# Converting a unit's blocks of g to hi and lo one unit later in the program text

## The chip, the core and the metric

The kernel runs on one core of a Trainium2 chip. The metric is the time of one execution in device microseconds (us); smaller is better. The core's engines run side by side, each taking its own instructions in order: PE (TensorE, matrix products into PSUM), ACT (ScalarE), DVE (VectorE), POOL (GpSimd, which cannot reach PSUM) and SP, which issues the DMA transfers.

## The reference

Attention in chunks of 64 tokens, then a feed-forward layer with the activation h - tanh(h), all in float32:

```python
scores = scale * np.matmul(q_c, k_c.transpose(0, 1, 2, 4, 3))   # chunks of 64 x 64
scores = scores - np.max(scores, axis=-1, keepdims=True)
attn = np.exp(scores)
attn = attn / (np.sum(attn, axis=-1, keepdims=True) + 1e-09)
out = np.matmul(attn, v_c)
...
h = x @ w_in          # x: 4608 x 512, w_in: 512 x 2048
g = h - np.tanh(h)
return (g @ w_out).astype(np.float32)   # w_out: 2048 x 512
```

q, k and v are 8 batches x 8 heads x 576 tokens x 64.

## The kernel before

The 4608 tokens are cut into nine groups of 512. Groups 0 to 2 run the feed-forward layer in a plain form (`FeedForward`); groups 3 to 8 run it in the class `Fast`, which the change touches. While a group's feed-forward layer runs, the attention of the next group is computed in between: `interleaved` puts its parts (splits of q, k and v into two float16 halves, scores, exponents, normalisation, a transposition by DMA, values) into lists `at[...]` that the loop of `Fast.run` calls at set steps.

To keep float32 accuracy with float16 products, each operand is held as two float16 numbers, "hi" (the rounded value) and "lo" (the rest).

A group in `Fast` is worked in 16 units: two halves `b` of 256 tokens, times eight pairs `j` of hidden blocks. One step `s` of `Fast.run` handles a unit:

- `gemm1` (L576): the first layer, 24 matmuls of 256 columns into one PSUM buffer `ph` (there are two).
- `shrink`: tanh on ACT (L584), `u` = h - tanh(h) on DVE (L585), three sums on POOL (L586 to L588) that make seven blocks out of the four of `u` (as in Strassen's scheme, seven products stand for eight), hi on ACT (L589) and lo on DVE (L590). `u` has two places; hi and lo have five sets of places, used in turn. The unit then goes into `queue`.
- the attention parts in `at[2 * s]`.
- `gemm2` (L607): the second layer, 21 matmuls, of the unit at the head of the queue, once more than `FAST_LAG` = 3 are queued: the unit of three steps earlier. When the unit at the head is the first of a half (`j == 0`), one step is left out and the next step runs two second layers.
- the attention parts in `at[2 * s + 1]`.

The second layer's products of a half add up in four PSUM tiles `po`. After the eighth unit of a half, `gemm2` calls `finish` (L611 to L633): two activations on ACT (L622 of the first PSUM tile, L623 of half the second), six scalar-tensor-tensor adds on DVE (all at L620, in the helper `add`), two subtractions or additions on POOL (L625 and L631), and two output DMAs. The next half's first second layer writes the same PSUM tiles, so it waits for these reads. With the lag of three, the finish of a group's first half falls in step 10 and that of its second half in step 2 of the next group; the last one falls behind the last unit.

In this part of the kernel the order on each engine is not written out by hand. The program text gives each instruction a rank; when the program is built, a planner goes through it with a clock of its own and sets the order in every engine's queue. On the chip each engine then keeps to that order. The lines of other work that share the engines with the units: L107, L124 (largest values of the next group's q, k and v), L114 (a reduction over partitions on POOL), L297 and L298 (splits into hi and lo), L308 (attention products), L321 to L323 (maxima, differences, exponents), L329 to L340 (normalisation, and hi and lo of the weights), L348 (the transposing DMA), L360 and L361 (attention's result).

Of the kernel before, what the change touches and what calls it, by code (L numbers as in the profile page):

```python
# [17 lines left out]
AF = mybir.ActivationFunctionType  # L18
ALU = mybir.AluOpType
# [3 lines left out]
P = 128  # L23
# [14 lines left out]
MOST = max(SIZES) * P  # L38
LAG = 2
FAST = 3  # L40
FAST_LAG = 3
RAW = 3
WS = 2
EARLY_FC = 8
# [15 lines left out]
def attn_ffn_kernel(ctx: ExitStack, tc: tile.TileContext, qE, kE, vE, qL, kL, vL, w_in, w_out, out):  # L60
# [8 lines left out]
    nc = tc.nc  # L69
    scale = 1.0 / math.sqrt(D)  # L70
# [18 lines left out]
    def place_of(a, part, fc, dtype=F16):  # L89

        return w_pool[fc].tile([P, DM], F32R, name=f"w{a}{part}{fc}").bitcast(dtype)
# [66 lines left out]
    class Early:  # L158
# [3 lines left out]
        def __init__(self, pool, psum, bufs, zeros):  # L162
            self.pool, self.psum, self.st, self.bufs = pool, psum, defaultdict(dict), bufs
            self.qbd, self.vbd = (
                [pool.tile([P, 4, P, 2], F32, name=f"{n}{i}", bufs=1) for i in range(bufs)] for n in ("qbd", "vbd")
            )
            for i in range(bufs):
                for t in self.qbd[i], self.vbd[i]:
                    for r, o in ((slice(0, D), slice(D, P)), (slice(D, P), slice(0, D))):
                        if t is self.qbd[i]:  # L170
                            nc.vector.memset(t[r, :, o], 0.0)
                        else:
                            nc.scalar.copy(out=t[r, :, o], in_=zeros[r].rearrange("p (hp d two) -> p hp d two", hp=4, two=2))
# [78 lines left out]
    class Late:  # L252
# [31 lines left out]
        def split(self, g, b, n):  # L284

            d, to = self.st[g, b], self.st[f"g{g}"]["to"][:, "qkv".index(n):"qkv".index(n) + 1]
            d["exp"] = self.st[f"g{g}"]["exp"]
            raw = self.raw[n][:, 2 * b:2 * b + 2].rearrange("p e n -> p (e n)")
            if n == "k":
                hl = self.k16  # L290
                if hl is None:
                    t = self.pool.tile([P, 2, 2 * H * CH], F16, name="a", bufs=1)
                    hl = t[:, 0], t[:, 1]
                d["k"] = hl
            else:
                hl = self.q16 if n == "q" else self.v16
            nc.scalar.activation(hl[0], raw, AF.Copy, scale=to)  # L297
            nc.vector.scalar_tensor_tensor(out=hl[1], in0=raw, scalar=to, in1=hl[0], op0=ALU.mult, op1=ALU.subtract)  # L298
# [172 lines left out]
    class FeedForward:  # L471
# [27 lines left out]
        def shrink(self):  # L499
            fc, t0, t1, n, ph = self.ph  # L500
            t = ffn.tile([P, MOST], F32, name="t", bufs=3)[:, :n]
            if self.half:
                nc.scalar.activation(t, ph, AF.Tanh, scale=self.sig)
                nc.vector.scalar_tensor_tensor(out=t, in0=ph, scalar=self.sig, in1=t, op0=ALU.mult, op1=ALU.subtract)  # L504
            else:
                nc.scalar.activation(t, ph, AF.Tanh)
                nc.vector.tensor_sub(t, ph, t)
            gh = ffn.tile([P, MOST], F32R, name="gh")[:, :n]
            gl = ffn.tile([P, MOST], F32R, name="gl")[:, :n]
            nc.scalar.copy(out=gh, in_=t)  # L510
            nc.vector.tensor_sub(gl, t, gh)  # L511
            self.queue.append((fc, t0, t1, (gh, gl)))
# [36 lines left out]
    class Fast:  # L549
# [5 lines left out]
        SUM = {7: 0, 3: 1, 4: 2, 6: 3, 5: 4, 2: 5, 1: 6}  # L555

        def __init__(self, pools):
            self.pools, self.queue, self.units, self.po = pools, [], 0, None
            u = xpool.tile([P, KC, MOST], F32R, name="xl").bitcast(F32).rearrange("p a n -> p (a n)")
            self.u = [u[:, i * 8 * P:i * 8 * P + 7 * P].rearrange("p (s n) -> p s n", n=P) for i in range(2)]  # L560
            tiles = [ffn.tile([P, MOST], F32R, name=f"g{a}").bitcast(F16) for _ in range(2) for a in "hl"] + g_tiles
            self.g = [[t[:, :7 * P].rearrange("p (s n) -> p s n", n=P) for t in tiles[2 * i:2 * i + 2]] for i in range(FAST_LAG + 2)]

# [13 lines left out]
                        k += 1  # L577

        def shrink(self, b, j):
            sig, to = self.powers[:2]  # L580
            t = ffn.tile([P, MOST], F32, name="t", bufs=3).rearrange("p (s n) -> p s n", n=P)
            u, (gh, gl) = self.u[self.units % 2], self.g[self.units % len(self.g)]
            self.units += 1
            nc.scalar.activation(t, self.ph, AF.Tanh, scale=sig)  # L584
            nc.vector.scalar_tensor_tensor(out=u[:, :4], in0=self.ph, scalar=sig, in1=t, op0=ALU.mult, op1=ALU.subtract)  # L585
            nc.gpsimd.tensor_add(u[:, 4:6], u[:, 1:3], u[:, 0:4:3])  # L586
            nc.gpsimd.tensor_add(u[:, 6], u[:, 1], u[:, 2])  # L587
            nc.gpsimd.tensor_sub(u[:, 0:4:3], u[:, 0:2], u[:, 2:4])  # L588
            nc.scalar.activation(gh, u, AF.Copy, scale=to)  # L589
            nc.vector.scalar_tensor_tensor(out=gl, in0=u, scalar=to, in1=gh, op0=ALU.mult, op1=ALU.subtract)  # L590
            self.queue.append((b, j, gh, gl, self.powers, self.row + 2 * b * P))

        def first_next(self):
            return self.queue[0][1] == 0
# [40 lines left out]
        def run(self, g, x, at):  # L635
            self.group(g, x)
            waited = False
            for s in range(2 * FC // 2):
                unit = divmod(s, FC // 2)
                self.gemm1(*unit)  # L640
                self.shrink(*unit)
                for f in at.pop(2 * s, []):
                    f()
                if len(self.queue) > FAST_LAG:
                    if self.first_next() and not waited:
                        waited = True
                    else:
                        waited = False
                        self.gemm2()
                        if len(self.queue) > FAST_LAG and not self.first_next():  # L650
                            self.gemm2()
                for f in at.pop(2 * s + 1, []):
                    f()
            for k in sorted(at):
                for f in at[k]:
                    f()

        def drain(self):
            while self.queue:
                self.gemm2()  # L660

# [2 lines left out]
    outs, g_tiles, post = [], [], []  # L664
# [63 lines left out]
    pools = []  # L728
# [17 lines left out]
    att, half, over = Late(late), Half(late), defaultdict(list)  # L746
    for g in range(1, NG):
        x, nx = nx, new_half_x() if g + 1 < NG else None
        at = interleaved(att, g + 1, nx) if nx else {}
        if g == 1:  # L750
            half.powers()
            first_place = late.tile([P, DM], F32, name="first_place", bufs=1).bitcast(F16)
            for fc in range(FC):

                at[2 * fc + 1].append(lambda fc=fc: half.convert(fc, place_of("l", 0, fc - 1) if fc else first_place))

            def more(k):

                if k == 0:
                    t = [place_of("h", 0, fc) for fc in range(4)]  # L760
                    att.q16, att.v16 = t[0:2], t[2:4]
                else:
                    outs.extend(place_of("h", 0, fc, F32) for fc in range(4, 8))
                    g_tiles.extend(place_of("h", 0, fc) for fc in range(8, 12))
                    half.free = [("h", 0, 12), ("h", 0, 13), ("h", 0, 14), ("h", 0, 15)]

            at[8].insert(0, lambda: more(0))
            at[2 * FC + 2].append(lambda: more(1))
        if g < FAST:
            if g == FAST - 1:  # L770
                for j in range(FC // 2):
                    at[4 * j + 7].append(lambda j=j: half.combine(j))
                    k = 4 * j + 9
                    (at if k < 2 * (FC + LAG) else over)[k].append(lambda j=j: half.shorten(j))
            order = range(FC) if g < FAST - 1 else [j + f * FC // 2 for j in range(FC // 2) for f in range(2)]
            ff = FeedForward(g, x)
            ff.room(ps_o1, range(2))
            ff.room(ps_o2, range(2, SIZES[g]))
            ff.run([(fc, 0, SIZES[g]) for fc in order], at)
            continue  # L780
        if g == FAST:
            for fs in over.values():
                for f in fs:
                    f()
            post.extend(place_of(*n, F32) for n in half.free[:3])
            g_tiles.extend(place_of(*n) for n in half.free[3:5])
            fast = Fast((ps_o1, ps_o2))
        fast.run(g, x, at)
    fast.drain()
# [46 lines left out]
```

## Time and profile before

| | |
|---|---|
| median of three runs | 953.4 us (952.98 to 954.25) |
| the profiled execution | 954.0 us, span of the profile 952.2 us |
| `Fast` on the time line | from about 348 us to the end |
| granted clock of TensorE, mean | 0.971 |
| busy share of the span: PE, DVE, ACT, POOL | 89%, 64%, 50%, 28% |

Times on a time line are microseconds from the span's start. A row of a time line has the start, the duration, the engine, the line, the operation with its output and inputs, shapes, and in brackets how long the engine sat idle before it and what ended that. Neighbouring instructions of an engine overlap a little: the next one starts some 0.1 us ahead of the end of the last. A row of waits has who waited, for whom, the sum in us, how many times, and the longest. A row of windows has a stretch, its length, the busy time and the number of instructions of PE, weight loads, DVE, ACT and POOL, then the granted clock, the DMA engines' share and GB/s. In the names, hi and lo lie in tiles `gh`, `gl`, `wh` or `wl`, and `u` in `xl`.

### The profile page before, as it was taken

How to read it: one execution, taken by the hardware profiler on the slowest of the kernel's cores; microseconds unless marked ns; L12 is line 12 of the kernel's file. 1: busy time of each engine (PE TensorE's matmuls, PEld its weight loads, DVE VectorE, ACT ScalarE, POOL GpSimd, SP SyncE). 2: the span in 40 equal slices, each digit the busy share in tenths (PEclk: the TensorE clock that was granted, in tenths of full speed). 3: DMA queues.
4: the chain of work that ended last, by engine and by line, in shares of the span. 5: the costliest groups of instructions: out<-in, count | busy, mean ns of one | idle time of the engine just before them, and what ended most of it. 6: DMA issues, size and time to landing. Idle time of an engine off the chain costs nothing.

```text
span 952.2 us, 19954 instructions
## 1 busy us (share of the span) xinstructions
PE 847.2 (89%) x8525; PEld 694.3 (73%) x8525; DVE 606.1 (64%) x878; ACT 472.9 (50%) x767; POOL 268.9 (28%) x375
## 2 busy tenths in 40 slices
PE   8999999999998768887887989879887889889997
PEld 5888778887665557776776877768776678778886
DVE  6987978776787756565646556565646555554343
ACT  7796967656454634335443543335433534433332
POOL 0000000000455463232423242332323242333342
PEclk9999999999999979999998999999999999999999
DMA  8764433113120322103021122112130101010000
GB/s 260 216 188 168 142 126 118 47 43 108 50 67 1 63 72 40 52 24 89 31 60 45 24 67 67 45 45 67 46 60 31 23 23 23 2 46 4 21 23 23
DMA packets 61400, 63.14 MB, mean 66 GB/s; under 512 B 32640, under 2 KB 40832, under 8 KB 61312
## 3 DMA queue, kind: packets, MB, share of 16 engines
q1 hardware_dynamic: 61312, 61.88, 22.4%
q8 instruction: 66, 1.08, 0.5%
q14 instruction: 22, 0.18, 0.1%
HBM read 45.09 MB, written 9.44 MB: 57 GB/s over the span
## 4 chain that ended last, share of the span: by engine, by line
PE 30%; DVE 28%; POOL 16%; ACT 12%; DMA 7%; issue 5%; SPq 2%; ACTq 0%; DVEq 0%; POOLq 0%
PE ph L495 10%; PE po L519 10%; DVE xl L585 5%; POOL xl L586 5%; POOL xl L588 5%; ACT wh L589 4%; DMA s<-a 4%; PE po L607 4%; DVE wh L590 4%; PE ph L576 3%; POOL xl L587 3%; ACT gh L589 3%; DVE gl L590 3%; DVE wh L298 2%; DVE a L298 1%
## 5 line engine op out<-in xcount | busy, mean ns | idle before, releaser
L576 PE MATMUL ph<-xh,wl 128*128 128x256 f16 x2160 | 262.2, 280 | 38.5 <-DVE xl L585 38.4
L576 PEld LDWEIGHTS <-wl 128*128 128x128 f16 x2160 | 215.8, 100 | 72.5 <-issue 42.2
L586 POOL TENSOR_TENSOR xl<-xl 128x256 f32<-128x256 f32 x96 | 69.5, 724 | 346.9 <-DVE xl L585 290.9
L590 DVE SCALAR_TENSOR_TENSOR wh<-xl,to_g,wh 128x896 f16<-128x896 f32 x57 | 66.5, 1167 | 130.0 <-ACT wh L589 130.0
L607 PEld LDWEIGHTS <-wh 128*128 128x128 f16 x1197 | 120.7, 101 | 36.3 <-issue 18.9
L589 ACT ACTIVATE wh<-xl,to_g 128x896 f16<-128x896 f32 x57 | 59.4, 1042 | 172.6 <-POOL xl L588 167.3
L607 PE MATMUL po<-wl,wh 128*128 128x256 f16 x642 | 107.2, 277 | 10.9 <-DVE wh L620 7.4
L607 PE MATMUL po<-wh,wh 128*128 128x256 f16 x555 | 105.8, 288 | 4.3 <-DVE wh L620 4.3
L590 DVE SCALAR_TENSOR_TENSOR gl<-xl,to_g,gh 128x896 f16<-128x896 f32 x39 | 46.3, 1187 | 84.7 <-ACT gh L589 84.7
L589 ACT ACTIVATE gh<-xl,to_g 128x896 f16<-128x896 f32 x39 | 40.6, 1042 | 117.9 <-POOL xl L588 112.7
L519 PE MATMUL po<-wh,gh 128*128 128x512 f32 x192 | 79.4, 414 | 4.4 <-ACT gh L510 4.4
L585 DVE SCALAR_TENSOR_TENSOR xl<-ph,sig,t 128x512 f32<-128x512 f32 x96 | 70.9, 739 | 18.5 <-ACT t L584 18.5
L495 PE MATMUL ph<-xh,wl 128*128 128x512 f16 (+2 forms) x324 | 77.0, 375 | 4.3 <-DVE t L504 3.2
L519 PE MATMUL po<-wh,gl 128*128 128x512 f32 x192 | 76.3, 401 | 0.5 <-DVE gl L511 0.4
L519 PE MATMUL po<-wl,gh 128*128 128x512 f32 x192 | 76.0, 396 | 0.0
L588 POOL TENSOR_TENSOR xl<-xl 128x256 f32<-128x256 f32 x96 | 70.5, 735 | 0.0
L607 PEld LDWEIGHTS <-gh 128*128 128x128 f16 x546 | 54.2, 100 | 19.0 <-issue 11.9
L584 ACT ACTIVATE t<-ph,sig 128x512 f32<-128x512 f32 x96 | 64.4, 671 | 1.0 <-PE ph L576 1.0
L607 PE MATMUL po<-wl,gh 128*128 128x256 f16 x292 | 45.4, 276 | 7.0 <-DVE wh L620 4.7
L511 DVE TENSOR_TENSOR gl<-t,gh 128x512 fp32r<-128x512 f32 (+1 forms) x52 | 37.4, 720 | 19.5 <-ACT gh L510 17.3
L587 POOL TENSOR_TENSOR xl<-xl 128x128 f32<-128x128 f32 x96 | 48.3, 504 | 0.0
L519 PEld LDWEIGHTS po<-wh,gh 128*128 128x128 f32 x192 | 36.5, 190 | 14.1 <-ACT gh L510 5.8
(146 smaller groups left out, 1409.5 us busy)
## 6 DMA issues: line engine op xcount, KB each, us to landing
raw<-w_in SPq DMA_DIRECT2D x16, 512.0 KB, 3.7
raw<-w_out SPq DMA_DIRECT2D x16, 512.0 KB, 5.5
out<-wh SPq DMA_DIRECT2D x32, 256.0 KB, 2.0
rawk<-kL SPq DMA_DIRECT2D x28, 256.0 KB, 3.3
rawv<-vL SPq DMA_DIRECT2D x28, 256.0 KB, 3.0
xl<-qL SPq DMA_DIRECT2D x28, 256.0 KB, 2.8
qbd<-qE SPq DMA_DIRECT2D x16, 128.0 KB, 4.3
k<-kE SPq DMA_DIRECT2D x8, 256.0 KB, 4.8
```

What stands on the lines that cost most here:

```text
L495: nc.tensor.matmul(ph, lhsT=self.weight(fc, 0, a)[:, kc * P:(kc + 1) * P], rhs=x[b][:, kc, cols], start=(k == 0), stop=(k == 3 * KC - 1))
L511: nc.vector.tensor_sub(gl, t, gh)
L519: nc.tensor.matmul(self.po[t], lhsT=gg[a][:, ts], rhs=self.weight(fc, 1, b), start=(fc == 0 and i == 0), stop=(fc == FC - 1 and i == 2))
L576: nc.tensor.matmul(self.ph[:, 1 - f::2, :], lhsT=half_w[fc][:, w, kc * P:(kc + 1) * P], rhs=rhs, start=(k == 0), stop=(k == 3 * KC - 1))
L584: nc.scalar.activation(t, self.ph, AF.Tanh, scale=sig)
L585: nc.vector.scalar_tensor_tensor(out=u[:, :4], in0=self.ph, scalar=sig, in1=t, op0=ALU.mult, op1=ALU.subtract)
L586: nc.gpsimd.tensor_add(u[:, 4:6], u[:, 1:3], u[:, 0:4:3])
L587: nc.gpsimd.tensor_add(u[:, 6], u[:, 1], u[:, 2])
L588: nc.gpsimd.tensor_sub(u[:, 0:4:3], u[:, 0:2], u[:, 2:4])
L589: nc.scalar.activation(gh, u, AF.Copy, scale=to)
L590: nc.vector.scalar_tensor_tensor(out=gl, in0=u, scalar=to, in1=gh, op0=ALU.mult, op1=ALU.subtract)
L607: nc.tensor.matmul(place[m], lhsT=part[:, self.SUM[m]], rhs=w[m][:, o], start=first, stop=(j == FC // 2 - 1 and part is gl), skip_group_ch ...
```

## The change

`shrink` ends after the three sums and keeps the unit in `ready`. A new function `split` makes hi and lo of the kept unit and puts it into the queue. In `run`, the step of a unit first issues the unit's own first layer, tanh, u and sums, then `split` for the unit before; the attention parts and the second layer follow as they did. `drain` splits the last unit. `FAST_LAG` goes from 3 to 2, so the second layer of a unit stays at the same step, and the sets of places for hi and lo go from five to four; two tiles that served the fifth set are no longer taken.

```diff
-FAST_LAG = 3
+FAST_LAG = 2
...
         def shrink(self, b, j):
-            sig, to = self.powers[:2]
+            sig = self.powers[0]
...
-            u, (gh, gl) = self.u[self.units % 2], self.g[self.units % len(self.g)]
-            self.units += 1
+            u = self.u[self.units % 2]
             nc.scalar.activation(t, self.ph, AF.Tanh, scale=sig)
             nc.vector.scalar_tensor_tensor(out=u[:, :4], in0=self.ph, scalar=sig, in1=t, op0=ALU.mult, op1=ALU.subtract)
             nc.gpsimd.tensor_add(u[:, 4:6], u[:, 1:3], u[:, 0:4:3])
             nc.gpsimd.tensor_add(u[:, 6], u[:, 1], u[:, 2])
             nc.gpsimd.tensor_sub(u[:, 0:4:3], u[:, 0:2], u[:, 2:4])
-            nc.scalar.activation(gh, u, AF.Copy, scale=to)
-            nc.vector.scalar_tensor_tensor(out=gl, in0=u, scalar=to, in1=gh, op0=ALU.mult, op1=ALU.subtract)
-            self.queue.append((b, j, gh, gl, self.powers, self.row + 2 * b * P))
+            self.ready = u, self.g[self.units % len(self.g)], (b, j), self.powers, self.row + 2 * b * P
+            self.units += 1
+
+        def split(self):
+            if not self.ready:
+                return
+            u, (gh, gl), unit, powers, row = self.ready
+            self.ready = None
+            nc.scalar.activation(gh, u, AF.Copy, scale=powers[1])
+            nc.vector.scalar_tensor_tensor(out=gl, in0=u, scalar=powers[1], in1=gh, op0=ALU.mult, op1=ALU.subtract)
+            self.queue.append((*unit, gh, gl, powers, row))
...
                 self.gemm1(*unit)
+                before, self.ready = self.ready, None
                 self.shrink(*unit)
+                before, self.ready = self.ready, before
+                self.split()
+                self.ready = before
                 for f in at.pop(2 * s, []):
...
         def drain(self):
+            self.split()
             while self.queue:
                 self.gemm2()
...
-            g_tiles.extend(place_of(*n) for n in half.free[3:5])
```

More of the change, by code (lines that the diff above doesn't have):

```diff
@@ L557, in __init__ @@
         def __init__(self, pools):
-            self.pools, self.queue, self.units, self.po = pools, [], 0, None
+            self.pools, self.queue, self.units, self.ready, self.po = pools, [], 0, None, None
             u = xpool.tile([P, KC, MOST], F32R, name="xl").bitcast(F32).rearrange("p a n -> p (a n)")
```

## The prediction

> **What bounds the kernel now.** I read the page's busy shares and its chain, the waits, the fast stage cut by group (windows), then the timelines of ACT, DVE and PE round one unit. A "unit" is one pass of the fast stage; its links are tanh (L584), u (L585), three sums (L586 to L588), hi (L589), lo (L590).
>
> ```profile
> span 952.2 us, 19954 instructions
> PE 847.2 (89%) x8525; PEld 694.3 (73%) x8525; DVE 606.1 (64%) x878; ACT 472.9 (50%) x767; POOL 268.9 (28%) x375
> PE 30%; DVE 28%; POOL 16%; ACT 12%; DMA 7%; issue 5%; SPq 2%; ACTq 0%; DVEq 0%; POOLq 0%
> PE ph L576 <- DVE xl L585: 39.8, 32, 7.6
> 551.70:656.60 104.90, 89.88 (x1109) 76.35 (x1107) 60.92 (x82) 44.66 (x54) 34.53 (x54) 0.95 0.18 51
> 857.50:952.00 94.50, 86.48 (x785) 76.50 (x783) 39.02 (x54) 31.11 (x41) 36.46 (x57) 0.99 0.05 18
> ```
>
> No engine is full: TensorE is busy 89%, yet the chain gives it only 30%, and it idles 39.8 us because u has not freed its PSUM buffer. The fifth row is one whole group, 16 units, 104.9 us from hi to hi.
>
> ```profile
> 563.12 1.04 ACT L589 ACTIVATE wh<-xl,to_g 128x896 f16<-128x896 f32 x1 [3.21 <-POOL xl L588]
> 564.07 0.67 ACT L584 ACTIVATE t<-ph,sig 128x512 f32<-128x512 f32 x1
> 564.64 0.68 ACT L622 ACTIVATE wh<-po,undo_g 128x512 f32<-128x512 f32 x1
> 567.95 1.04 ACT L589 ACTIVATE wh<-xl,to_g 128x896 f16<-128x896 f32 x1 [2.63 <-POOL xl L588]
> 568.90 0.46 ACT L623 ACTIVATE wh<-po,undo_g 128x256 f32<-128x256 f32 x1
> 569.25 0.68 ACT L584 ACTIVATE t<-ph,sig 128x512 f32<-128x512 f32 x1
> 574.34 1.04 ACT L589 ACTIVATE gh<-xl,to_g 128x896 f16<-128x896 f32 x1 [4.41 <-POOL xl L588]
> ...
> 567.19 0.73 POOL L588 TENSOR_TENSOR xl<-xl 128x256 f32<-128x256 f32 x1
> ...
> 889.25 2.78 PE L576 MATMUL ph<-xh,wl 128*128 128x256 f16 x24
> 894.16 1.04 PE L576 MATMUL ph<-xh,wl 128*128 128x256 f16 x8
> ```
>
> ACT runs hi, then the next tanh, so the units form a loop: hi, tanh, u behind lo on DVE, sums, hi. It closes in 567.95 - 563.12 = 4.83 us when nothing else is inside. A TensorE unit takes 894.16 - 889.25 = 4.91. Without intruders TensorE would set the pace at 16 x 4.91 = 79 us a group plus the attention's products; at 104.9 the intruders in the loop decide, microsecond for microsecond. The next hi came after 574.34 - 567.95 = 6.39: 1.56 lost, at a place where a finish (L620 to L631) runs.
>
> **What the change does to the order.** Hi and lo of a unit are issued in the text after the next unit's tanh, u and sums. If the engines followed the text, tanh would leave hi's shadow in every unit. They do not:
>
> ```profile
> 352.93 0.67 ACT L584 ACTIVATE t<-ph,sig 128x512 f32<-128x512 f32 x1
> 354.59 0.69 ACT L584 ACTIVATE t<-ph,sig 128x512 f32<-128x512 f32 x1 [0.99 <-PE ph L576]
> 356.81 1.04 ACT L589 ACTIVATE gh<-xl,to_g 128x896 f16<-128x896 f32 x1 [1.53 <-POOL xl L588]
> ...
> 643.02 1.91 ACT L107 ACTIVATE a<-xl 128x2048 uint8<-128x2048 f32 x1 [1.12 <-DMA s<-a]
> ```
>
> L107 belongs to the next group in the text, two units on, and runs here ahead of two units of the present group. At 354.59 a tanh already stands ahead of the hi that the text has first; there no second layer lies between two first layers. So the planner puts in each queue what its own clock has ready, and the text only breaks ties. With a second layer between (2.3 us) the sums are ready first and hi goes ahead: all plain units show it. I expect hi before tanh there after the change too, and price that move at nothing; its cover is that readiness, and without it the second rival holds.
>
> Ties do change, and they lie at the finish. On ACT above, L622 is followed by hi and only then by L623, which needs nothing but products that are long there; text order put hi first. In the new text the finish (issued with the second layer of its step) comes before hi. DVE in the same stretch:
>
> ```profile
> 565.93 0.48 DVE L620 SCALAR_TENSOR_TENSOR wh<-po,undo_g,wh 128x256 f32<-128x256 f32 x1
> 569.03 1.15 DVE L590 SCALAR_TENSOR_TENSOR wh<-xl,to_g,wh 128x896 f16<-128x896 f32 x1 [2.62 <-ACT wh L589]
> 570.09 0.48 DVE L620 SCALAR_TENSOR_TENSOR wh<-po,undo_g,wh 128x256 f32<-128x256 f32 x1
> 571.27 0.48 DVE L620 SCALAR_TENSOR_TENSOR wl<-po,minus_g,wl 128x256 f32<-128x256 f32 x1
> 571.66 0.74 DVE L585 SCALAR_TENSOR_TENSOR xl<-ph,sig,t 128x512 f32<-128x512 f32 x1
> 572.32 0.48 DVE L620 SCALAR_TENSOR_TENSOR wh<-po,minus_g,wl 128x256 f32<-128x256 f32 x1
> ...
> 617.98 0.47 DVE L620 SCALAR_TENSOR_TENSOR wh<-po,undo_g,wh 128x256 f32<-128x256 f32 x1
> 621.07 1.15 DVE L590 SCALAR_TENSOR_TENSOR wh<-xl,to_g,wh 128x896 f16<-128x896 f32 x1 [2.61 <-ACT wh L589]
> 623.71 1.21 DVE L321 TENSOR_REDUCE mx<-psa 128x16 f32<-128x1024 f32 x1
> 625.23 1.21 DVE L322 TENSOR_TENSOR s<-psa,mx 128x1024 f32<-128x1024 f32 x1
> 626.36 0.74 DVE L585 SCALAR_TENSOR_TENSOR xl<-ph,sig,t 128x512 f32<-128x512 f32 x1
> ```
>
> One add runs, DVE idles 2.62 us for hi, then lo, then four adds (570.09 to 571.66) in front of u, which is in the loop.
>
> **The change part by part.**
> 1. L623 ahead of hi: it moves into ACT's 2.63 us wait (565.3 to 565.7; hi cannot start before the sum of 567.19 ends). Tanh then starts 0.35 earlier, but u follows DVE, so this pays only through the adds.
> 2. Finish at step 2 (groups 2 to 5 of six; the sixth below). With L623 done near 565.7, four adds, 0.39 apart ((571.66 - 570.09)/4), fill 566.3 to 567.9, inside the wait. The last add depends on the one before; the planner slips a ready operation between such a pair (u stands there now), so I let lo go between, and the last add after lo: u at 569.03 + 1.06 + 0.39 = 570.48 against 571.66, 1.18 us gained. Ends: 0 (order kept) and 1.57 (last add also ahead); I take 1.18, as the row of the present slip is nearest.
> 3. Finish at step 10 (groups 1 to 5): lo 621.07, then last add 0.39, L321 and L322 1.13 each, u at 621.07 + 1.06 + 0.39 + 2.26 = 624.78 against 626.36: 1.57 gained. Ends: 0, and 4.2 if L321 and L322 too go ahead of lo. I take 1.57: L321 needs scores that end late.
> 4. Last group: few intruders, TensorE leads by little, so its own waits count:
>
> ```profile
> 877.52 0.60 PE L607 MATMUL po<-wh,gh 128*128 128x256 f16 x4
> 884.34 0.93 PE L576 MATMUL ph<-xh,wl 128*128 128x256 f16 x7
> 919.05 0.60 PE L607 MATMUL po<-wh,wh 128*128 128x256 f16 x4
> 924.46 0.71 PE L576 MATMUL ph<-xh,wl 128*128 128x256 f16 x5
> ...
> 887.36 1.04 ACT L589 ACTIVATE wh<-xl,to_g 128x896 f16<-128x896 f32 x1 [3.20 <-POOL xl L588]
> 622.88 0.72 POOL L631 TENSOR_TENSOR wh<-wh,wl 128x256 f32<-128x256 f32 x1
> ```
>
> Two second layers, 42 matmuls at (4.91/45 =) 0.109, are 4.58 us; they took 6.82 and 5.41, waiting for adds: 2.24 + 0.83 = 3.07. With the adds inside the earlier wait both go; the loop, 1.18 shorter twice, nearly follows. I take 3.07; ends 0 and 3.07.
> 5. Queue of two instead of three: a unit enters it a step later, so the second layer of unit s-3 still follows the first layer of s. Nothing moves on TensorE. Hi and lo have two steps instead of three to be ready: a unit's lo comes some 6 us after its tanh, two loops are 9.7; covered.
> 6. Four sets: hi of s overwrites what the second layer of s-4 reads. Tightest after a finish: that layer is the first of the pair that starts at 877.52 and is over before 884.34; its overwriter is the hi at 887.36. Three us spare at least; nothing. If the spare went, hi, tanh, u and sums would wait in turn, and TensorE on u. Two tiles fewer cost no instruction, and no DMA, SP or POOL instruction moves; L625 and L631 come earlier, behind the same sums. The adds will now run beside the sums; L631 amid the four adds between 621.07 and 623.71 took 0.72, as the sum at 567.19 took 0.73, so I expect neither to stretch.
>
> Sum: 4 x 1.18 + 5 x 1.57 + 3.07 = 15.6. The profiled execution took 954.0 (span 952.2 and 1.8 around it), 0.6 above the median of 953.4. 954.0 - 15.6 - 0.6 = 937.8, so 938.
>
> **The rivals.**
> - *Finish order kept.* If L623 is not ready in the plan when L622 ends, hi keeps its place and the time stays 953.4. For it: the plan's clock is not in the trace. Against: its products end two matmuls after L622's.
> - *Tanh ahead of hi in every unit*, as the text reads. The loop then breaks and TensorE sets the pace: between 79 us a group and its busy 89.9 against 104.9, so 15 to 26 saved, in five groups 75 to 130; the attention's own chain through ACT and DVE stays, so I take the lower end: 879. Against: the 354.59 row and every plain unit.
> - *TensorE sets the time already.* Then the loop's late places are covered and only step 4 pays: 950.3. The Trainium skill ("Perfetto Trace Analysis", Identifying the Most-Contended Engine) has the engine of highest occupancy optimised first, for TensorE judged by weight loads; by that rule the change, which leaves TensorE's work alone, brings next to nothing. The trace disagrees: weight loads 73%, and TensorE waits for u.
> - *Slower: hi, now last of its step, falls behind an attention cast that is late on the chip.* Place:
>
> ```profile
> 581.50 1.04 ACT L589 ACTIVATE gh<-xl,to_g 128x896 f16<-128x896 f32 x1 [2.62 <-DVE sm L332]
> 584.95 1.04 ACT L339 CAST a<-s 128x1024 f16<-128x1024 f32 x1 [2.41 <-DVE s L333]
> 585.90 0.68 ACT L584 ACTIVATE t<-ph,sig 128x512 f32<-128x512 f32 x1
> ```
>
> With L339 first, hi starts at 585.90 and tanh 0.95 later than now; where tanh does not wait for L339 today, up to 4.4. Five groups: 5 to 22 us, 958 to 975, likeliest 959. It outweighs the finish from 3.1 us a group on. For it: L339 now precedes hi in the text. Against: it needs L333, which runs behind lo here.
>
> **How the numbers follow.** Forecast (finish order flips) 0.60; order kept 0.14; every tanh ahead 0.07; TensorE bound 0.03; slower 0.16. About 0.2% (1.9 us) is what a measurement of this kernel can tell from no change. Faster: 0.60 + 0.07 + 0.03 = 0.70; same 0.14; slower 0.16. The likeliest case alone runs from 923 (4 x 1.57 + 5 x 4.2 + 3.07 = 30) to 950 (last-group waits only). The range 923 to 958 adds the kept order and the mild slower end; it leaves out the 879 and the rest of the slower case.
>
> **What would show it.** Right: L623 directly behind L622; five L620 before lo; u right after lo and one add; lo to u after a finish at 1.45 and 3.7 us (now 571.66 - 569.03 = 2.63 and 626.36 - 621.07 = 5.29); hi still before tanh in plain units; no wait of second-layer matmuls for L620 in the last group. Wrong: L623 still behind hi; tanh before hi in plain units (far faster); L339 or another attention operation newly in front of hi or u; hi waiting for TensorE (the four sets).

## The result, and the profile after

The changed kernel takes 945.5 us (four runs, 943.8 to 946.9) against 953.2 before: ratio 0.9916, interval 0.9894 to 0.9938. The direction and the place of the gain were as forecast (938.0, range 923 to 958); its size was half. The profiled execution took 946.9 with a span of 944.3, so 7.9 less than the span of before, against a forecast sum of 15.6. Times are medians of a kernel's runs; one of the ten runs of the kernel with the delay alone took 3326.8 us, for no reason that the record shows, and is left out of its time.

The page after, first its busy shares and its chain by engine, then the first row of the waits of PE; the last two rows are the largest wait of the second layer for the adds, before (L607) and after (L614):

```profile
span 944.3 us, 19977 instructions
PE 849.3 (90%) x8525; PEld 700.0 (74%) x8525; DVE 611.3 (65%) x878; ACT 473.3 (50%) x767; POOL 263.3 (28%) x375
PE 32%; DVE 25%; POOL 14%; ACT 12%; issue 8%; DMA 7%; SPq 2%; ACTq 0%; DVEq 0%; POOLq 0%
PE ph L576 <- DVE xl L584: 46.1, 32, 3.6
PE po L607 <- DVE wh L620: 19.2, 21, 1.3
PE po L614 <- DVE wh L627: 3.9, 6, 0.7
```

Nothing has changed in kind. TensorE still carries a third of the chain and still waits for u, now 46.1 us where it was 39.8. The adds of the finish held the second layer up for 25.0 us before (19.2 and, in a second row, 5.8) and hold it up for 3.9 now; but the waits for attention values (L308, for the transposing DMA) grew from 19.3 to 25.7 as well, so most of what TensorE no longer waits at the finish it waits elsewhere. The loop of hi, tanh, u and sums still sets the pace.

The places where the time was won are the finishes. (Lines of the changed kernel: tanh L583, u L584, sums L585 to L587, hi L596, lo L597, adds L627, the finish activations L629 and L630, the finish's POOL operations L632 and L638.) ACT, DVE and POOL at the finish of step 2, and DVE at that of step 10, after:

```profile
562.54 0.68 ACT L629 ACTIVATE wh<-po,undo_g 128x512 f32<-128x512 f32 x1
563.11 0.47 ACT L630 ACTIVATE wh<-po,undo_g 128x256 f32<-128x256 f32 x1
565.85 1.04 ACT L596 ACTIVATE wh<-xl,to_g 128x896 f16<-128x896 f32 x1 [2.27 <-POOL xl L587]
...
563.83 0.87 DVE L627 SCALAR_TENSOR_TENSOR wh<-po,undo_g,wh 128x256 f32<-128x256 f32 x2
565.39 0.48 DVE L627 SCALAR_TENSOR_TENSOR wl<-po,minus_g,wl 128x256 f32<-128x256 f32 x1
566.92 1.33 DVE L597 SCALAR_TENSOR_TENSOR wh<-xl,to_g,wh 128x896 f16<-128x896 f32 x1 [1.05 <-ACT wh L596]
568.17 0.47 DVE L627 SCALAR_TENSOR_TENSOR wh<-po,minus_g,wl 128x256 f32<-128x256 f32 x1
568.57 0.74 DVE L584 SCALAR_TENSOR_TENSOR xl<-ph,sig,t 128x512 f32<-128x512 f32 x1
...
565.09 0.73 POOL L587 TENSOR_TENSOR xl<-xl 128x256 f32<-128x256 f32 x1
565.77 0.73 POOL L632 TENSOR_TENSOR wl<-wh,wh 128x256 f32<-128x256 f32 x1
566.58 0.72 POOL L638 TENSOR_TENSOR wh<-wh,wl 128x256 f32<-128x256 f32 x1
...
618.17 1.33 DVE L597 SCALAR_TENSOR_TENSOR wh<-xl,to_g,wh 128x896 f16<-128x896 f32 x1 [1.05 <-ACT wh L596]
622.20 0.74 DVE L584 SCALAR_TENSOR_TENSOR xl<-ph,sig,t 128x512 f32<-128x512 f32 x1
```

L630 stands right behind L629, the five adds run inside the wait for hi, lo comes next, then the sixth add, then u. From the start of lo to u is 568.57 - 566.92 = 1.65 us at step 2 (before 2.63) and 622.20 - 618.17 = 4.03 at step 10 (before 5.29). Measured from tanh to tanh, the gains are the same in every group that has such a finish, within 0.01: 0.98 at step 2 in four groups and 1.26 at step 10 in five, 10.2 us.

And a place where time was lost: ACT at step 13, before and then after.

```profile
636.79 0.68 ACT L584 ACTIVATE t<-ph,sig 128x512 f32<-128x512 f32 x1
640.86 1.04 ACT L589 ACTIVATE gh<-xl,to_g 128x896 f16<-128x896 f32 x1 [3.39 <-POOL xl L588]
646.96 0.67 ACT L584 ACTIVATE t<-ph,sig 128x512 f32<-128x512 f32 x1
```

```profile
632.64 0.68 ACT L583 ACTIVATE t<-ph,sig 128x512 f32<-128x512 f32 x1
638.82 1.91 ACT L107 ACTIVATE a<-xl 128x2048 uint8<-128x2048 f32 x1 [5.50 <-issue]
640.73 1.02 ACT L596 ACTIVATE gh<-xl,to_g 128x896 f16<-128x896 f32 x1
643.56 0.67 ACT L583 ACTIVATE t<-ph,sig 128x512 f32<-128x512 f32 x1
...
635.95 0.72 POOL L587 TENSOR_TENSOR xl<-xl 128x256 f32<-128x256 f32 x1
```

The unit's last sum is over at 636.67, but the first of the two L107 is now in front of hi, and it starts only at 638.82. Its row names no releaser; the kernel before has L107 wait for the transposing DMA to have read tile `a`, and here the last of those transfers ends at 638.17. Hi comes at 640.73. From tanh to tanh the step takes 10.92 us where it took 10.17; four groups have this, 0.86 + 0.78 + 0.75 + 0.81 = 3.2 us.

The third part of the account is the last group. Before, then after: the first layer of its first unit, that unit's tanh, and the last product of the kernel.

```profile
858.85 1.47 PE L576 MATMUL ph<-xh,wl 128*128 128x256 f16 x12
862.66 0.67 ACT L584 ACTIVATE t<-ph,sig 128x512 f32<-128x512 f32 x1
945.96 0.27 PE L607 MATMUL po<-wl,gl 128*128 128x256 f16 x1
```

```profile
854.00 1.47 PE L576 MATMUL ph<-xh,wl 128*128 128x256 f16 x12
855.57 0.69 ACT L583 ACTIVATE t<-ph,sig 128x512 f32<-128x512 f32 x1
938.06 0.27 PE L614 MATMUL po<-wl,wh 128*128 128x256 f16 x1
```

From that tanh to the end of the last product it is 83.57 us before and 82.76 after: 0.8 gained. Sum: 10.2 + 0.8 - 3.2 = 7.8, against the 7.9 that the spans differ. That it comes out so close is partly luck: single steps elsewhere moved by up to 0.8 us either way, 0.4 lost in all, and the first tanh of `Fast` comes 0.5 earlier.

### The profile page after: what moved, and what is told of

It reads as the page before. It is cut to its first block, busy times and chain, and to the rows that moved or that the text cites. A ratio compares the mean times of both kernels' runs of the same rounds, so it can differ in the third digit from the quotient of the medians.

```text
span 944.3 us, 19977 instructions
## 1 busy us (share of the span) xinstructions
PE 849.3 (90%) x8525; PEld 700.0 (74%) x8525; DVE 611.3 (65%) x878; ACT 473.3 (50%) x767; POOL 263.3 (28%) x375
## 4 chain that ended last, share of the span: by engine, by line
PE 32%; DVE 25%; POOL 14%; ACT 12%; issue 8%; DMA 7%; SPq 2%; ACTq 0%; DVEq 0%; POOLq 0%
PE ph L495 10%; PE po L519 9%; PE ph L576 6%; PE po L614 5%; POOL xl L587 4%; DVE xl L584 4%; DMA s<-a 4%; POOL xl L585 4%; ACT wh L596 4%; ACT gh L596 3%; DVE gl L597 3%; POOL xl L586 3%; DVE wh L597 2%; DVE wh L298 2%; DVE a L298 1%
## 5 line engine op out<-in xcount | busy, mean ns | idle before, releaser
L576 PE MATMUL ph<-xh,wl 128*128 128x256 f16 x2160 | 271.3, 286 | 45.5 <-DVE xl L584 45.3
L585 POOL TENSOR_TENSOR xl<-xl 128x256 f32<-128x256 f32 x96 | 70.3, 733 | 357.0 <-DVE xl L584 293.2
L597 DVE SCALAR_TENSOR_TENSOR gl<-xl,to_g,gh 128x896 f16<-128x896 f32 x48 | 55.3, 1152 | 131.6 <-ACT gh L596 131.6
L596 ACT ACTIVATE gh<-xl,to_g 128x896 f16<-128x896 f32 x48 | 50.0, 1041 | 145.2 <-POOL xl L587 134.7
L597 DVE SCALAR_TENSOR_TENSOR wh<-xl,to_g,wh 128x896 f16<-128x896 f32 x48 | 59.1, 1231 | 80.3 <-ACT wh L596 80.2
L596 ACT ACTIVATE wh<-xl,to_g 128x896 f16<-128x896 f32 x48 | 50.0, 1042 | 119.7 <-POOL xl L587 119.7
L614 PEld LDWEIGHTS <-wh 128*128 128x128 f16 x1008 | 98.6, 98 | 11.4
L614 PE MATMUL po<-wl,wh 128*128 128x256 f16 x576 | 91.6, 273 | 0.0
L614 PE MATMUL po<-wh,wh 128*128 128x256 f16 x432 | 78.5, 273 | 0.0
L584 DVE SCALAR_TENSOR_TENSOR xl<-ph,sig,t 128x512 f32<-128x512 f32 x96 | 71.0, 740 | 7.7 <-ACT t L583 7.7
L614 PEld LDWEIGHTS <-gh 128*128 128x128 f16 x672 | 65.7, 98 | 12.9 <-issue 4.9
L587 POOL TENSOR_TENSOR xl<-xl 128x256 f32<-128x256 f32 x96 | 71.4, 744 | 0.0
L583 ACT ACTIVATE t<-ph,sig 128x512 f32<-128x512 f32 x96 | 64.6, 673 | 3.9 <-PE ph L576 3.6
L614 PE MATMUL po<-wh,gh 128*128 128x256 f16 x336 | 55.7, 274 | 3.9 <-DVE wh L627 3.9
L308 PEld LDWEIGHTS <-wh 64*64 64x64 f16 x2688 | 27.4, 112 | 34.1 <-issue 33.7
L614 PE MATMUL po<-wl,gh 128*128 128x256 f16 x336 | 52.4, 273 | 0.0
```

Of the source, the lines that this page charges most:

```text
L576: nc.tensor.matmul(self.ph[:, 1 - f::2, :], lhsT=half_w[fc][:, w, kc * P:(kc + 1) * P], rhs=rhs, start=(k == 0), stop=(k == 3 * KC - 1))
L596: nc.scalar.activation(gh, u, AF.Copy, scale=powers[1])
L597: nc.vector.scalar_tensor_tensor(out=gl, in0=u, scalar=powers[1], in1=gh, op0=ALU.mult, op1=ALU.subtract)
L614: nc.tensor.matmul(place[m], lhsT=part[:, self.SUM[m]], rhs=w[m][:, o], start=first, stop=(j == FC // 2 - 1 and part is gl), skip_group_ch ...
```

## The experiments

**Hi and lo in their own step, behind the second layer.** The text order that lets the finish come first, without the delay by a unit; queue and sets as in the change.

```diff
-                before, self.ready = self.ready, None
                 self.shrink(*unit)
-                before, self.ready = self.ready, before
-                self.split()
-                self.ready = before
...
                         if len(self.queue) > FAST_LAG and not self.first_next():
                             self.gemm2()
+                self.split()
```

> Hi and lo of a unit stay in the unit's own step of the text, only behind that step's second layer (and finish) instead of ahead of it; the queue still holds two. Theory 'finish order' (the gain comes from L623 and the five adds standing ahead of hi and lo after a half's last product, and the unit's delay itself does nothing): as the changed kernel, 945 within 2 us. Rival 'a unit later' (the gain comes from hi and lo standing behind the next unit's tanh and u): back to the kernel before, 953.

Measured: 945.0 us, ratio 0.9909 (0.9893 to 0.9926), the same as the change. What moved the time is that the finish stands ahead of hi in the text; delaying the split by a unit does nothing of its own.

**The queue alone.** The kernel before with the lag of two and four sets.

```diff
-FAST_LAG = 3
+FAST_LAG = 2
...
-            g_tiles.extend(place_of(*n) for n in half.free[3:5])
```

> The kernel before with only the shorter queue (two) and four sets of places; hi and lo where they were, so the second layer and each finish come one step earlier. Theory 'finish order': hi still precedes L623 and lo the adds, so no gain from there: 953 within 4 us, the shift of the finishes by a step being the unknown. Rival 'the queue did it': 945.

Measured: 962.3, ratio 1.0088 (1.0073 to 1.0103): 8.4 us slower, outside what I gave it. The finishes move to steps 1 and 9, and the planner's order of everything round them changes. ACT of this kernel at its step 12:

```profile
633.91 1.04 ACT L339 CAST a<-s 128x1024 f16<-128x1024 f32 x1 [2.90 <-DVE s L333]
634.86 0.68 ACT L584 ACTIVATE t<-ph,sig 128x512 f32<-128x512 f32 x1
```

The attention's cast L339 now stands in front of this tanh and waits for L333; the tanh comes 9.91 us after the one before it, where it was 8.68 before. That is the slower rival's mechanism, in another kernel and at tanh instead of hi. It is one place only: before, L339 stood in the next step, and that step is now shorter, so the 8.4 us are not accounted for row by row.

**The delay alone.** The change with the old lag of three and the fifth set: second layers one step later.

```diff
-FAST_LAG = 2
+FAST_LAG = 3
...
+            g_tiles.extend(place_of(*n) for n in half.free[3:5])
```

> Edit: the change with the old queue length (three) and the old number of sets, so the second layers come a whole step later than before: a finish at steps 3 and 11. Theory (the time of the loop depends on which operations stand in it at the finish, not on the queue's length as such): hi still behind both finish activations; the planner's order puts L321 and L322 ahead of the five adds at one finish and splits the adds round L329 at the other, so I expect no more than a few us either way: 940 to 955, likeliest 947. Rival (the queue's length sets it, a shorter one being slower as in the queue-alone run, 962, so a longer one faster): below 938.

Measured: 954.05, the median of nine runs (952.5 to 955.5), ratio 1.0009 (0.9999 to 1.0019), at the slow end of my range. With the queue-alone run this says that neither half of the change is a gain by itself, and that a longer queue is not better as such. A second layer at another step lets the planner lay the finish and the attention in another order: in one group, from tanh to tanh, step 3 takes 8.32 us where it took 7.07 before, step 4 0.57 for 9.58 and step 5 10.33 for 7.08. Which of these orders costs what was not separated.

**Tanh first in every unit.** The change, with hi of a unit held behind the next unit's tanh.

```diff
-            nc.scalar.activation(t, self.ph, AF.Tanh, scale=sig)
+            self.tanh = nc.scalar.activation(t, self.ph, AF.Tanh, scale=sig)
...
-            nc.scalar.activation(gh, u, AF.Copy, scale=powers[1])
+            with tc.issue_after(self.tanh.ins):
+                nc.scalar.activation(gh, u, AF.Copy, scale=powers[1])
```

> The changed kernel, with an issue-order edge that keeps hi of a unit behind the next unit's tanh on ACT (no wait, order alone), so that the order of the text really holds in every unit. Theory 'the loop hi, tanh, u, sums, hi sets the pace': the loop opens, and the time falls towards TensorE's: 880, between 865 and 905. Rival 'TensorE sets the pace already': 943 to 946, as the changed kernel.

Measured: 888.9, ratio 0.9319 (0.9305 to 0.9334). The chain by engine, the group that took 103.16 us after the change (from its first tanh to that of the next group, 552.34 to 655.50), and some ACT rows in it:

```profile
PE 53%; DVE 18%; issue 8%; ACT 8%; POOL 6%; DMA 6%; SPq 1%; ACTq 0%; DVEq 0%; POOLq 0%
532.30:625.23 92.93, 86.50 (x1109) 75.58 (x1108) 64.58 (x82) 44.55 (x56) 40.89 (x54) 0.97 0.20 56
535.50 0.69 ACT L583 ACTIVATE t<-ph,sig 128x512 f32<-128x512 f32 x1 [1.31 <-PE ph L576]
537.68 1.04 ACT L597 ACTIVATE gh<-xl,to_g 128x896 f16<-128x896 f32 x1 [1.50 <-POOL xl L587]
540.41 0.69 ACT L583 ACTIVATE t<-ph,sig 128x512 f32<-128x512 f32 x1 [1.68 <-PE ph L576]
```

In these rows tanh waits for TensorE, and the units stand 540.41 - 535.50 = 4.91 us apart: TensorE's pace, not the loop's. So the loop was the bound, and the rival "TensorE sets the time already" falls. By the Trainium skill ("Perfetto Trace Analysis", Identifying the Most-Contended Engine) the engine with the highest occupancy is the one to optimise first. The trace agrees only in part: TensorE has it (90% after the change), but the 57 us came from reordering two ACT instructions per unit with TensorE's instructions as they were. Its wait for u fell from 46.1 to 28.1 us, all its idle time from 95.0 to 58.7, and its busy time from 849.3 to 829.3 at a mean granted clock of 0.984 instead of 0.965.

**L107 behind hi.** The change, with each L107 held behind the hi in front of which it had slipped.

```diff
-                spread(junk, some, d["sums"][:, "qkv".index(n):"qkv".index(n) + 1])
+                with tc.issue_after(his[-3].ins) if len(his) > 2 else nullcontext():
+                    spread(junk, some, d["sums"][:, "qkv".index(n):"qkv".index(n) + 1])
...
-            nc.scalar.activation(gh, u, AF.Copy, scale=powers[1])
+            his.append(nc.scalar.activation(gh, u, AF.Copy, scale=powers[1]))
```

> The changed kernel with one order edge: the two L107 of the next group stand behind the hi of unit 13, as in the kernel before, and not one ahead of it. Theory 'new intruder' (in four groups hi and tanh wait for L107 and its transposing DMA; tanh to tanh there grew from 10.1 to 10.9 us): 4 x 0.8 = 3.2 us less, 942. Rival 'covered' (the later stretches of the group, or TensorE in the last group, give it back): 945, no change.

Measured: 941.9, ratio 0.9871 (0.9853 to 0.9889), 3.5 us below the change. ACT at step 13:

```profile
634.61 1.04 ACT L597 ACTIVATE gh<-xl,to_g 128x896 f16<-128x896 f32 x1 [3.38 <-POOL xl L588]
636.74 1.91 ACT L107 ACTIVATE a<-xl 128x2048 uint8<-128x2048 f32 x1 [1.09 <-DMA s<-a]
```

Hi no longer stands behind L107, which waits for the DMA after it, and the step is back at 10.14 us in this group. The four groups give back 3.1 us in the trace, and the interval lies just below the change's. The price of the slip is thus shown.

**No POOL work beside lo.** The first POOL operation of the finish (L632) is left out and L638 takes e1 in its place; nothing else in the order changes. The output then lacks a term, so this kernel serves for its times alone.

```diff
-            nc.gpsimd.tensor_sub(q, e1, e5)
...
-            nc.gpsimd.tensor_add(oa[:, :HD], p, q)
+            nc.gpsimd.tensor_add(oa[:, :HD], p, e1)
```

> Edit: the first POOL operation of the finish (L632, 0.73 us) is left out and L638 takes e1 in its place (so one head's block of the output lacks a term); POOL is then done with L638 before lo starts. The order of all else is the same. Theory (lo is slower because POOL works beside it): lo after the finish takes 1.15 again, not 1.33, and u follows it 1.45 us after its start at step 2 (now 1.65) and 3.8 at step 10 (now 4.03); 9 finishes inside the loop by 0.2 is 1.8 us: 943.7 against 945.5. Rival (lo is slower for the add that follows it, or because five adds precede it): lo stays at 1.33, time 945.5.

Measured: 942.2, ratio 0.9889 (0.9873 to 0.9904). DVE at the finish of step 2:

```profile
564.79 1.15 DVE L597 SCALAR_TENSOR_TENSOR wh<-xl,to_g,wh 128x896 f16<-128x896 f32 x1 [1.05 <-ACT wh L596]
566.26 0.74 DVE L584 SCALAR_TENSOR_TENSOR xl<-ph,sig,t 128x512 f32<-128x512 f32 x1
```

Lo takes 1.15 again, and u follows 1.47 us after its start, the 1.45 of the forecast. The tanh-to-tanh distance at the finish falls by 0.18 (step 2) and 0.17 (step 10), 1.6 us over nine. The time fell by 3.3, more than that, but its interval overlaps the change's: the rows show the 1.6, the time alone would not.

**Dummy products in TensorE's idle stretch.** After the change, TensorE stands still for 4.24 us before the last attention values (839.45 to 843.69), and the granted clock then falls to 0.50; the next first layer takes 4.89 us instead of 2.79. Fourteen products into the free PSUM tile fill the first 3.18 us of the stretch.

```diff
+            if g == NG - 1 and b == 1:
+                for _ in range(14):
+                    nc.tensor.matmul(ps[:, 0].rearrange("p hp e q -> p (hp e q)"), lhsT=half_w[0][:, 0, :P], rhs=half_w[0][:, 0], start=True, stop=True)
             self.products(lambda c, e, hp: ps[:, c, hp, e],
```

> Edit: 14 dummy products of 128x512 into the attention's free PSUM tile ahead of the last group's last values (L308), so that TensorE is busy in the stretch in which it stood still for 4.24 us (839.45 to 843.69); everything else stands in the same order on every engine. At the row of an L519 product of 128x512 (0.39 to 0.41 us fp32, an f16 one about half: 0.21) they fill about 3 us. Slow-clock theory: the granted clock fell to 0.50 because of the idle stretch and cost 1.07 (the L308 group took 2.05 instead of 0.98) and 2.09 (the next first layer took 4.88 instead of 2.79); with the stretch filled the clock stays at 1.00 there, the two take 0.98 and 2.79, and the time falls by 3.2 from the 946.9 of the profiled run: about 942.5 to 943.5, with the runs closer together than before (943.8 to 946.9). Rival (the clock falls for the transfers that run at that moment, DMA share 1.00, and not for the idle stretch): the clock falls to 0.50 all the same and the time stays 945.5, or rises by what the dummies delay, up to 3.

Measured: 943.1 (941.6 to 946.3), ratio 0.9900 (0.9881 to 0.9918), which overlaps the change's interval; the profiled run is the slowest of the five. Two windows of PE behind the dummies, columns: stretch, length, PE busy, granted clock, DMA share, GB/s:

```profile
844.00:846.00 2.00, 0.77 (x73) 1.00 0.68 129
846.00:848.00 2.00, 2.00 (x56) 0.61 0.00 0
```

The clock fell to 0.50 all the same, only later (some 0.4 us into the second of these stretches), so neither theory held as written: the dummies ended at 843.33, and the 3 us behind them, with two short bursts of attention products in them, were enough. No transfer runs when it falls (DMA share 0.00). The Trainium skill ("TensorE: Matmul & The Clock Gate", What's actually happening) has the clock halved after an idle window of about 3.4 us that runs on its own count. The traces agree in the level, 0.50, and in the count: in each of the twelve traces all stretches at 0.50 start at the same phase of a period of 3.413 us, and each lasts one to four such periods, but for the one that begins behind the last product. Here the slow stretch is 6.83 us long after the change (843.17 to 850.00) and 3.41 with the dummies (846.44 to 849.85). So it matters what falls into a whole period: none of TensorE's work did in the one ahead of 843.17, and 1.51 us did in the one ahead of 846.44. In the kernel before, a stretch of the same kind (849.55 to 852.62) left the clock at 1.00; the period that ends in it, at 851.89, holds 1.64 us. How much is enough is not shown. The phase differs from trace to trace, which may be part of the spread of the change's runs; that was not tested and stays open.

**The places that the change left free.** With tanh first, tile `a` is still shared by L107, the k split and the transposition. The run with both gives L107 and the k split places of their own:

```diff
+            att.junk = place_of(*half.free[3], U8).rearrange("p (a n) -> p a n", n=H * CH)
+            att.k16 = [place_of(*n) for n in half.free[4:6]]
```

> Edit: tanh first in every unit (as in e3), and besides the places that the change left free are used: the output of L107 that nobody reads goes into one, the k split of L297 and L298 into two others, so that neither waits for the transposes (DMA s<-a) to have read tile a. Theory (with the loop broken TensorE sets the pace, and what is left are its waits, 28 us for u and 11 us for values in e3, which come from attention work that stands waiting for that tile in front of tanh): the waits go in part; ends 850 (all 39 us gone) and 889 (nothing), I expect 872. Rival (the waits come from the amount of work on ACT and DVE, which stays): 889 as e3.

Measured: 891.7, ratio 0.9363 (0.9330 to 0.9397): no gain over 888.9. The waits had moved, so two runs took the lines one by one.

> Edit: the other half: tanh first in every unit, L107 writes into a place of its own, the k split goes through tile a as before. Theory (L114 in front of the sums): POOL stands in L114 while the sums of step 9's unit wait, and the second layer waits for hi (L597) as in the run with both, 3 to 5 us in each of four groups; what L107 no longer waits for is gained: 888 to 893, likeliest 890. Rival: no wait of the second layer for hi, and the time falls below 885.

> Edit: tanh first in every unit, and of the two uses of the free places in the run with both only one: the k split (L297, L298) gets its own places; L107 writes tile a as before. Theory (in the run with both, the early L107 made its maximum over the partitions, L114 on POOL, come in front of the sums of the unit with the first finish activation, so that its hi, and the second layer behind it, came 5 us late; the k split's own place does no harm): L114 stays where it was, the second layer's waits for hi are gone, and of the 28 us of waits for u in the tanh-first run those of the k split go, some 6 us: 882, range 876 to 889. Rival (more attention work between tanh and u is what costs, wherever L114 stands): 889 or above.

Measured: 907.1 with L107's place alone (0.9521, 0.9497 to 0.9546) and 880.2 with the k split's places alone (0.9231, 0.9209 to 0.9252). POOL with L107's place, and PE's waits there:

```profile
497.61 0.38 POOL L114 PARTITION_ALL_REDUCE xtop<-sums  x1 [5.87 <-issue]
504.82 0.71 POOL L585 TENSOR_TENSOR xl<-xl 128x256 f32<-128x256 f32 x1 [6.82 <-DVE wh L298]
PE po L615 <- ACT gh L597: 15.2, 5, 5.3
```

Freed of its wait, L107 runs early, and with it the reduction L114, which now stands on POOL ahead of the sums of step 9's unit: those come at 504.82 although their u was over at 490.92. L114's own row is 0.38 us, but POOL runs nothing else from 491.74 to 504.82; in that time the trace has instructions named MODIFY_POOL_CONFIG at 491.9, ahead of L114, and at 498.0, behind it. The same is so in every group that has an L114, in the kernel before too (640.82 to 654.78), where it falls between the units of steps 13 and 14; what it costs there was not tested. The second layer waits 15.2 us for hi, as foreseen; that the whole costs 18 us over tanh first was not, and it is not accounted for. The k split's places alone are the best version here; the chain by engine and the same group as above:

```profile
PE 64%; DVE 14%; ACT 6%; issue 6%; DMA 5%; POOL 4%; SPq 1%; ACTq 0%; DVEq 0%; POOLq 0%
527.67:615.64 87.97, 83.17 (x1101) 73.51 (x1099) 64.62 (x82) 44.53 (x55) 43.48 (x54) 0.99 0.20 61
```

TensorE carries two thirds of the chain, and the group takes 88.0 us with 83.2 of them busy.

## Why the prediction was right, and where it was off

- *The loop sets the pace, and the planner keeps hi before tanh in plain units.* Right: every plain unit has that order after the change, and the tanh-first run shows what the order costs (57 us).
- *Part 1, L623 ahead of hi.* Right, at all finishes.
- *Parts 2 and 3, the adds at the finish.* The order came out as forecast. The terms were too large: 0.98 instead of 1.18 four times and 1.26 instead of 1.57 five times, 2.4 us in all. Some 0.18 of each is lo, which I priced at the 1.15 of the plain row while it took 1.33 beside L638; the run without POOL work beside lo gives that back. What is left at step 10 is about 0.1 us. Part 6 asked only whether adds and sums slow each other. They don't (L587 took 0.73 beside an add); but the finish's POOL operations, which come earlier, now lie beside lo. The trace of before had the row that tells it:

```profile
569.43 1.33 POOL L625 TENSOR_TENSOR wl<-wh,wh 128x256 f32<-128x256 f32 x1 [1.52 <-ACT wh L623]
```

  L625 started beside a lo in each of the eleven finishes that have one behind them and took 1.33 there; in the last finish, with no lo beside it, it took 0.72.
- *Part 4, the last group.* TensorE's waits went, exactly as sized: from its first product to its last the group took 85.64 us instead of 88.69. But 0.8 us reached the end, not 3.07. The step that failed is "TensorE leads by little, so its own waits count". Before, TensorE was done with the first unit's first layer at 860.32, 2.3 us ahead of the tanh that needs it; after, at 855.47, 0.1 ahead. It had spent that lead in the 4.24 us wait for values and at half clock behind it. From the first tanh on it now works without a gap at 4.91 a unit, which is slower than the loop's 4.82; the four kernels with tanh first, in which no loop holds it up, take the same 82.76 from that tanh to the last product. In the run with own-step hi and that with the dummies the loop sets this stretch, and it takes 82.35 and 82.18: of the 3.07, no more than 1.4 was to be had there with the loop as it is. How much of the 1.4 a run gets also depends on how long the clock is low ahead of it: the first layer behind the wait for values took 4.89 us in the change's trace and 4.35 in that of the own-step run, which was left a lead of 0.5. Where two bounds lie 2% apart, taking away the waits of one is worth only the distance to the other.
- *Part 5, nothing moves with the queue.* Right for the change, where the second layer stays at its step. The lone shorter queue shows how much hangs on that: 8.4 us.
- *The rivals.* That hi, now last of its step, falls behind an attention operation that is late on the chip was the slower rival, at 0.16. It happened, and together with the forecast: with L107 instead of L339, at step 13, 0.8 us in four groups, 3.2 in all. I had priced it only at L339 and let it stand as an alternative to the gain at the finish, when the two lie in different steps and can both come true. This and the terms above add up to 2.4 + 2.3 + 3.2 = 7.9, against the missing 15.6 - 7.9 = 7.7.

## What to carry to other kernels

Where a planner orders the queues by what its own clock has ready, moving a step in the text changes little but ties, as here: list the ties at the moved step and at every place where late work of another stage can slip in front of it, and price both. Before waits are counted as gain, look at how far the waiting engine leads the one that would set the pace next. If a loop through several engines sets the pace, breaking it with one enforced order (888.9 us, and 880.2 with a tile less shared) can be worth far more than clearing what stands inside it, as it was here (945.5).

## What the runs showed of the hardware

In these traces a DVE operation that reads two inputs from SBUF and a sum on POOL, which does so too, hold each other up, and the one that started first keeps its time. With tanh first, the two overlap in many units; DVE, then POOL:

```profile
532.43 1.62 DVE L598 SCALAR_TENSOR_TENSOR wh<-xl,to_g,wh 128x896 f16<-128x896 f32 x1 [1.09 <-ACT wh L597]
534.83 1.14 DVE L598 SCALAR_TENSOR_TENSOR wh<-xl,to_g,wh 128x896 f16<-128x896 f32 x1
532.38 0.73 POOL L587 TENSOR_TENSOR xl<-xl 128x256 f32<-128x256 f32 x1
534.99 1.56 POOL L585 TENSOR_TENSOR xl<-xl 128x256 f32<-128x256 f32 x1 [1.88 <-DVE xl L584]
```

The sum that started at 532.38 took its 0.73 and lo behind it 1.62; the lo that started at 534.83 took its 1.14 and the sum behind it 1.56. The Trainium skill ("SBUF — State Buffer", SBUF: two separate sides) describes a pair of ports that DVE and POOL lock in turn for a whole instruction. The trace agrees on who waits, and a DVE add with one input in PSUM and a sum beside it keep their times (0.48 and 0.73 us); the loss is a little under the overlap (0.47 for 0.68 us, 0.84 for 0.98, and 0.18 for 0.38 at the finish after the change).
